# Keeping w1 in its load tiles across the layer-1 forward and backward products, and shorter lives for wq and K tiles in the layer-1 backward attention

## The chip, the core and the metric

The kernel runs on one core of a Trainium2 chip. The metric is device time in microseconds of one launch. Times inside the program are given from the start of the profiled span.

## The reference, cut to what matters

Two layers are applied to a decode step of 2 sequences (D = 1024): attention over a cache of 16384 positions (32 query heads, 4 key/value heads, head size 128), then an MLP (F = 3584, tanh Gelu), each with a residual. Both layers use the same weights. The output and the gradients with respect to x, both caches and all weights are returned.

```python
x = A_x
x = x + _A_ref(_layernorm(x, axis=-1), A_k_cache, A_v_cache, A_wq, A_wo)
x = x + _B_ref(_layernorm(x, axis=-1), B_w1, B_b1, B_w2, B_b2)
x = x + _A_ref(_layernorm(x, axis=-1), A_k_cache, A_v_cache, A_wq, A_wo)
x = x + _B_ref(_layernorm(x, axis=-1), B_w1, B_b1, B_w2, B_b2)
```

_B_ref applies a second layer norm of its own, then h = gelu(y @ w1 + b1) and h @ w2 + b2. The backward pass needs, in layer 1, dh = (g @ w2.T) * gelu', then dh @ w1.T, two layer-norm backwards, the product with wo.T, the attention backward, the product with wq.T, and the same again for layer 0.

## The kernel before, in words

The two caches are 64 MB in all (2 sequences x 4 heads = 8 groups of 4 MB for K and as much for V), so they are streamed from memory. The unit of loading is a tile of 128 partitions x 4096 bf16, 1 MB. The pool `ld` has NLD = 7 such tiles. All loads are issued by the queue of SyncE (SP) in the order of the program (`w_take` L331 for weights, `kv_load` L469 for the caches, L961 and L986 for wq). A new tile takes, of the 7 buffers, the one whose last reader stands earliest in the program; its load waits on SP until that reader is done, and all loads after it on SP wait too. The order of every engine's instructions is written out by hand (the kernel opens a manual schedule); nothing is moved by a scheduler.

The stages follow each other: layer 0 forward, layer 1 forward, layer 1 backward, layer 0 backward with the output gradients.

Weights. `w_fwd` (L341) multiplies a vector by a weight matrix: it loads the tiles one by one and, on each, has PE make 32 small matmuls (`fwd_rows` L337) into the accumulator `acc_all`. w1 has 7 tiles (6 of 4 x 1024 columns, one of 8 x 512). The class `Back` (L361) multiplies by the transposed matrix. Its `load(k)` (L371) loads tile k and leaves four units in `todo[k]`; a unit turns a quarter of the tile in place, either on DVE (`turn32` L269, a transpose of 32 x 32 blocks, for rows below `nd`) or on PE (`turn` L358: eight 128 x 128 transposes into a PSUM tile, then a copy back by ACT, L159). `some(k, n)` runs n units, `prod(k)` the products of tile k (`products` L296 behind DVE-turned rows into `dm_d`, L418 behind PE-turned ones into `dm_p`), and `run()` goes over the tiles, turning tile k + 1 before the products of tile k. `open` makes the spread operand from dh (`spread_g` L278 and L281). `copies_on("A")` puts PSUM copies on ACT.

The layer-1 MLP. `mlp_hidden(1)` runs two layer norms, `w_fwd` over w1 (7 loads), adds b1 (`hpre` L830) and computes the Gelu (L832 to L846: Exp on ACT at L838, the rest on DVE). `mlp_slope(1)` (L859 to L869) computes the derivative of the Gelu, `mlp_hidden_bwd` (L874) dh. `weights_down(1)` (L876) then loads the 7 tiles of w1 again as a `Back`, multiplies, loads wo (8 tiles, also a `Back`), runs the two layer-norm backwards and multiplies by wo.

The layer-1 backward attention, `attn_bwd` (L645). It walks over slots; a slot is a quarter (8 x 128 positions) of a V tile: PE transposes it (`emit_T` L480), a copy brings it to SBUF, and two slots later PE makes dP from it (`score`, L726). After four slots `post` makes dS of the chunk on DVE (L698) and puts the products with the K tile of the same chunk into a queue: `quad` (L512), two halves for each K tile, each taken in a later slot. A K tile is loaded when its first quad is issued, except in the last group (index 6): there `post` loads it at once (`accs[g].pre[c] = kv_load(...)`), and at the last chunk `post` also issues the loads of the first five w2 tiles of the next stage (`ahead.load(k)`).

When both sequences of a key/value head are done, `wq_now` queues the product with that quarter of wq: in the next slot both its tiles are loaded, in slots +7 to +14 DVE turns them row by row, in slots +12 and +17 PE multiplies (L296), at +19 the sums are collected. The last quarter of wq (`wq_steps`, `wqL` below is its pair of tiles) is loaded and turned on PE from the second slot of the last group on, one step in every other slot (more often when over six wait), and multiplied at the very end (`products` L995), as its dq is known only then. The order of groups is 0, 4, 3, 1, 5, 2, 6, with group 7 (its tiles are held) in between; there are 128 slots, 112 to 127 being the last group. In the idle slots after the last V tile, units of w2 tile 0 are run (`ahead.some(0, 1)`).

After it come the product with w2 for layer 0 (`w2b`: a forward product for layer 1 and a transposed one in one pass), w1 and wo again, and the layer-0 attention backward with all stores.

## Time and profile before

| what | value |
|---|---|
| median of 3 runs | 1139.64 us (1136.17 to 1146.07) |
| profiled execution: span on the page (a time of its own beside the span is not given) | 1138.1 us |
| PE busy | 915.9 us, 80% |
| DVE, ACT busy | 619.8 us (54%), 534.0 us (47%) |
| POOL busy | 70.2 us, 6% |
| moved by DMA | 449.20 MB, mean 395 GB/s |
| read, written | 348.14 MB, 98.58 MB |
| chain that ended last, by engine | PE 45%, DMA 35%, DVE 10%, issue 5%, ACT 4% |
| loads of w1 and w2 tiles (in_B_w) | 42 of 1 MB, median 12.9 us to landing |

The page gives busy time for each engine, the span in 40 slices of 28.45 us, the DMA queues, and the chain of work that ended last: followed back from the last instruction, at each step to whatever released it. Busy shares are averages over all stages, so the stages that the change touches are read from the stretches and the timeline: layer-1 w1 lies at about 421 to 469 us, the layer-1 backward attention at about 490 to 666 us. A DMA's time in the chain runs from its issue to its landing and so holds the wait behind other transfers. In the timeline, the bracket at the end of a line is the idle time of that engine before the instruction and what ended it.

### The profile page before, as it was taken

How to read it: one execution, taken by the hardware profiler on the slowest of the kernel's cores; microseconds unless marked ns; L12 is line 12 of the kernel's file. 1: busy time of each engine (PE TensorE's matmuls, PEld its weight loads, DVE VectorE, ACT ScalarE, POOL GpSimd, SP SyncE). 2: the span in 40 equal slices, each digit the busy share in tenths (PEclk: the TensorE clock that was granted, in tenths of full speed). 3: DMA queues.
4: the chain of work that ended last, by engine and by line, in shares of the span. 5: the costliest groups of instructions: out<-in, count | busy, mean ns of one | idle time of the engine just before them, and what ended most of it. 6: DMA issues, size and time to landing. Idle time of an engine off the chain costs nothing.

```text
span 1138.1 us, 38123 instructions
## 1 busy us (share of the span) xinstructions
PE 915.9 (80%) x16766; PEld 674.7 (59%) x16767; DVE 619.8 (54%) x1363; ACT 534.0 (47%) x1356; POOL 70.2 (6%) x124
## 2 busy tenths in 40 slices
PE   4979795468888975789887678888898897899996
PEld 3867674358766754778765567755545454455552
DVE  1545451180545523654442246678798767786876
ACT  0544351005544420434333214468697766676764
POOL 0000000000000000000000000022121111111210
PEclk9988895567999875899998678999999978897978
DMA  8999999999999979999999699998999999999997
GB/s 371 423 425 425 424 424 413 395 413 423 423 425 423 412 288 404 388 422 421 399 413 393 232 380 309 370 386 302 403 419 421 421 419 424 423 411 421 423 385 290
DMA packets 104183, 449.20 MB, mean 395 GB/s; under 512 B 7238, under 2 KB 11334, under 8 KB 66896
## 3 DMA queue, kind: packets, MB, share of 16 engines
q1 hardware_dynamic: 86672, 354.46, 77.6%
q0 software_dynamic: 17344, 92.29, 19.6%
q8 instruction: 131, 2.15, 0.7%
q14 instruction: 36, 0.29, 0.1%
HBM read 348.14 MB, written 98.58 MB: 393 GB/s over the span
## 4 chain that ended last, share of the span: by engine, by line
PE 45%; DMA 35%; DVE 10%; issue 5%; ACT 4%; POOL 0%; SPq 0%; DVEq 0%; ACTq 0%; POOLq 0%
DMA kv_V<-in_A_v_cache_dram 13%; PE tp L480 10%; DMA wt<-in_B_w_dram 5%; PE acc_all L512 4%; PE tpm L1527 4%; DMA kv_K<-in_A_k_cache_dram 4%; PE xm L1336 4%; DMA wt<-in_A_wo_dram 3%; DMA out_dram<-keepK 3%; DMA keepK<-in_A_v_cache_dram 3%; PE sc L633 3%; PE xm L1250 2%; PE wtp L358 2%; PE dp L1389 2%; PE dp L726 2%
## 5 line engine op out<-in xcount | busy, mean ns | idle before, releaser
L159 ACT COPY kT<-tp 128x512 int32<-128x512 int32 x200 | 117.4, 587 | 298.4 <-PE tp L480 289.1
L162 DVE COPY kT<-tp 128x1024 bf16<-128x1024 bf16 x168 | 114.9, 690 | 141.8 <-PE tp L480 130.4
L480 PE MATMUL tp<-ident,kv_K 128*128 128x128 bf16 x1728 | 142.0, 230 | 6.9 <-DMA kv_K<-in_A_k_cache_dram 6.8
L480 PEld LDWEIGHTS <-kv_K 128*128 128x128 bf16 x1728 | 107.8, 103 | 7.7 <-DMA kv_K<-in_A_k_cache_dram 7.5
L170 DVE CAST big<-xm 128x512 bf16<-128x512 f32 x133 | 86.3, 684 | 19.3 <-PE xm L1336 14.3
L167 ACT CAST big<-xm 128x512 bf16<-128x512 f32 x151 | 82.1, 595 | 25.0 <-PE xm L1336 14.8
L633 PE MATMUL sc<-qT_bf,kT 128*128 128x8 bf16 x2048 | 91.5, 171 | 0.1
L633 PEld LDWEIGHTS <-kT 128*128 128x128 bf16 x2048 | 75.7, 97 | 26.7 <-issue 20.8
L337 PEld LDWEIGHTS <-wt 128*128 128x128 bf16 x1920 | 57.4, 104 | 54.7 <-issue 17.8
L167 ACT CAST keepV<-xm 128x512 bf16<-128x512 f32 (+1 forms) x137 | 75.0, 594 | 29.5 <-PE xm L1336 18.5
L480 PE MATMUL tp<-ident,kv_V 128*128 128x128 bf16 x864 | 70.2, 227 | 14.1 <-DMA kv_V<-in_A_v_cache_dram 12.2
L597 ACT ACTIVATE e_all<-sc,negm 128x64 bf16<-128x64 f32 x256 | 77.2, 343 | 1.0 <-DVE negm L592 1.0
L170 DVE CAST keepV<-xm 128x512 bf16<-128x512 f32 (+1 forms) x101 | 65.9, 684 | 18.9 <-PE xm L1336 12.7
L269 DVE STREAM_TRANSPOSE wt<-wt 128x512 int32<-128x512 int32 x104 | 63.6, 674 | 14.2 <-PE w2b_f L337 11.0
L512 PE MATMUL acc_all<-kv_V,e_all 128*16 128x256 bf16 x864 | 46.0, 293 | 28.7 <-DMA kv_V<-in_A_v_cache_dram 14.4
L159 ACT COPY wt<-wtp 128x512 int32<-128x512 int32 x72 | 40.3, 587 | 57.0 <-PE wtp L358 54.1
L480 PEld LDWEIGHTS <-kv_V 128*128 128x128 bf16 x864 | 55.2, 101 | 16.2 <-DMA kv_V<-in_A_v_cache_dram 13.1
L597 ACT ACTIVATION_READ_ACCUMULATOR e_all<-sc,negm 128x1 f32 x256 | 59.8, 234 | 0.0
L167 ACT CAST keepK<-xm 128x512 bf16<-128x512 f32 x98 | 53.0, 596 | 14.1 <-PE xm L1336 7.5
L1389 PE MATMUL dp<-wdo,kT 128*128 128x64 bf16 x896 | 52.8, 206 | 0.0
L358 PE MATMUL wtp<-ident,wt 128*128 128x128 bf16 x576 | 47.8, 244 | 4.9 <-ACT wt L159 2.6
L1336 PE MATMUL xm<-QmK,blk 64*128 64x512 bf16 x256 | 48.8, 444 | 2.3 <-ACT keepV L167 1.0
(387 smaller groups left out, 1564.4 us busy)
## 6 DMA issues: line engine op xcount, KB each, us to landing
kv_K<-in_A_k_cache_dram SPq DMA_DIRECT2D x81, 1024.0 KB, 13.0
kv_V<-in_A_v_cache_dram SPq DMA_DIRECT2D x81, 1024.0 KB, 12.9
wt<-in_B_w_dram SPq DMA_DIRECT2D x42, 1024.0 KB, 12.9
wt<-in_A_wo_dram SPq DMA_DIRECT2D x32, 1024.0 KB, 9.6
out_dram<-big POOLq DMA_DIRECT2D x26, 1024.0 KB, 18.9
out_dram<-keepV POOLq DMA_DIRECT2D x19, 1024.0 KB, 20.7
out_dram<-keepK POOLq DMA_DIRECT2D x17, 1024.0 KB, 17.8
wt<-in_A_wq_dram SPq DMA_DIRECT2D x16, 1024.0 KB, 11.0
```

Source lines behind the costliest of these rows:

```text
L159: S.copy(out=dst.bitcast(I32), in_=src.bitcast(I32))
L162: V.tensor_copy(out=dst, in_=src)
L167: S.copy(out=dst, in_=src)
L170: V.tensor_copy(out=dst, in_=src)
L269: V.transpose(out=w, in_=w)
L358: PE.transpose(tp[:, o, :], view[:, o * 128:(o + 1) * 128], ident[:])
L480: PE.transpose(tp[:, j, :], cv[:, b * 8 + j, :], ident[:])
L512: PE.matmul(self.acc[cg:cg + 16, :], lhsT=coef(u), rhs=self.cv[:, t:t + 2, :].rearrange("p t d -> p (t d)"), start=False, stop=True, tile_ ...
L597: S.activation(out=e_all[:, g, f * half:(f + 1) * half, l, h, :], in_=sc[g][f][:, h, :].rearrange("p (a b) -> p a b", b=2), func=ACT.Exp, ...
L633: PE.matmul(sc[g][f][:, :, t % TH], lhsT=kT[:, j, :], rhs=q_bf[:, g, :], start=True, stop=True)
L1336: PE.matmul(pss[k][:], lhsT=blk[p:p + 64, o + 2 * h + k // 2, :], rhs=Qm[p:p + 64, :, :].rearrange("p a b -> p (a b)"), start=True, stop=T ...
L1389: PE.matmul(dp[:, :, t:t + 4], lhsT=kT[:, j, :], rhs=wd[:, :, x:x + 4], start=(b + j == 0), stop=False)
```

## The change

Three things are changed.

1. w1 is loaded once for layer 1. `mlp_hidden(1)` gets the `Back` object; `w_fwd` with `keep` loads all 7 tiles through it, and after the forward product of tile k runs the turning units of tile k (all four, for the first six; for the last tile the two PE-turned ones, and its two DVE-turned ones later, one beside the Exp and one after the spread). Forward products go over the tiles in the order 1, 0, 3, 2, 5, 4, 6. `weights_down(1)` finds the tiles loaded and turned. The seven buffers are held from the loads to the products.
2. The Gelu of layer 1 and its derivative are computed in one chain that uses the square and 0.5 (1 + th) once; the write of `h_all` for layer 1 (`h1_out`) stands after the start of the backward product.
3. In `attn_bwd` the two wq tiles of a quarter are loaded four slots apart and each is turned and multiplied in the slots right after (slots +1/+4 to +7/+9 and +5/+8 to +11/+13, sum at +15); the last quarter is begun seven slots later and taken one step a slot; K tiles of the last group are loaded at their first quad; the five w2 loads stand in the queue behind the last K quad; one unit of w2 tile 0 stands ahead of the last wq product, the others follow after the attention.

```diff
--- before.py
+++ after.py
@@ -338,11 +338,22 @@
                           rhs=x[:, j0 + j, :].unsqueeze(1).to_broadcast([128, nw // 2, 2]),
                           start=False, stop=True, skip_group_check=True)
 
-    def w_fwd(W, n_in, n_out, x, between=None):
+    def w_fwd(W, n_in, n_out, x, between=None, keep=None):
         JO = n_out // 128
         nw = min(WIDE, 512 // JO)
         fps = ACCT[:, 0:JO * nw].rearrange("p (j b) -> p j b", b=nw)
         V.memset(fps, 0.0)
+        if keep is not None:
+            keep.fps, keep.x, keep.nw = fps, x, nw
+            for k in range(len(keep.tiles)):
+                keep.load(k)
+            for k in range(len(keep.tiles)):
+                keep.forward(k)
+                if k < len(keep.tiles) - 1:
+                    keep.some(k)
+            for _ in range(2):
+                keep.todo[k].pop()()
+            return fps[:, :, 0:2]
         for j0, nj, c0, cw in w_tiles(W, n_in, n_out):
             fwd_rows(fps, nw, w_take(W, j0, nj, c0, cw), x, j0, c0 // 128)
             if between:
@@ -367,6 +378,11 @@
             self.tiles = [tiles[i] for i in order]
             self.n_o, self.wv, self.todo = n_out // 128, {}, {}
             self.seen = set()
+            self.nw = None
+
+        def forward(self, k):
+            j0, nj, c0, cw = self.tiles[k]
+            fwd_rows(self.fps, self.nw, self.wv[k], self.x, j0, c0 // 128)
 
         def load(self, k):
             j0, nj, c0, cw = self.tiles[k]
@@ -374,7 +390,7 @@
             flat, per = wv.rearrange("p j n -> p (j n)"), max(1, 1024 // cw)
 
             def unit(u):
-                if self.fps is not None:
+                if self.fps is not None and self.nw is None:
                     fwd_rows(self.fps, WIDE, wv[:, u:u + 1], self.x, j0 + u, 0)
                 if j0 + u * per < self.nd:
                     turn32(flat[:, u * 1024:(u + 1) * 1024])
@@ -673,14 +689,13 @@
         def wq_now(kv):
             n = wq_job(kv)
             n[1]()
-            for f in n[0]:
-                sch.later(1, f)
-            for j in range(DJ):
-                sch.later(7 + j, n[2][j])
             for k in range(2):
-                sch.later(12 + 5 * k, n[3][k])
+                sch.later(1 + 4 * k, n[0][k])
+                for j in range(4):
+                    sch.later(4 + 4 * k + j, n[2][4 * k + j])
+                sch.later(9 + 4 * k, n[3][k])
             if kv == groups[-3] % HKV:
-                sch.later(19, wq_sum)
+                sch.later(15, wq_sum)
 
         def wq_sum():
             fin = px([128, DJ, 2], F32, "dn_fin")
@@ -704,18 +719,21 @@
                     done_g.append(g % HKV)
                     if g == groups[-1]:
                         wq_n["last"][1]()
+                        ahead.some(0, 1)
                         wq_n["last"][3]()
                     elif done_g.count(g % HKV) == 2:
                         wq_now(g % HKV)
                 accs[g] = Acc(g, "K", None, finish, 2 if g == G - 1 else groups.index(g) % 2)
             acc = accs[g]
-            if g == groups[-1]:
-                accs[g].pre[c] = kv_load("K", g, c)
+            coef = lambda u: ds[:, u - c * CP].rearrange("p h t -> p (h t)")
+            def queue():
+                queue_acc(sch, acc, [c], False, coef)
+                if g == groups[-1] and c == NCH - 1:
+                    sch.q.append(lambda: [ahead.load(k) for k in range(NLD - 2)])
                 if c == NCH - 1:
-                    for k in range(NLD - 2):
-                        ahead.load(k)
-            coef = lambda u: ds[:, u - c * CP].rearrange("p h t -> p (h t)")
-            sch.later(2, lambda: queue_acc(sch, acc, [c], c == NCH - 1, coef))
+                    queue_acc(sch, acc, [], True)
+
+            sch.later(1 if g == groups[-1] else 2, queue)
 
         def score(s):
             g, c, b = slots[s]
@@ -745,7 +763,7 @@
                     kTs[s] = emit_T(cv, b, True)
                     if s % 3 == 2 and s >= 8 and v_turns:
                         v_turns.popleft()()
-                if g == groups[-1] and b == 1 and c == 0:
+                if g == groups[-1] and b == 0 and c == 2:
                     n = wq_n["last"] = wq_steps(l, g % HKV, dqT, dn, lambda: pt([128, 8, 128], BF16, "wtq"),
                                                 lambda: px([128, 512], F32, "dn_ps"))
                     for k, f in enumerate(n[0]):
@@ -754,10 +772,8 @@
             sch.run_slot(1 if s < len(slots) else 2)
             if 2 <= s < len(slots) + 2:
                 score(s - 2)
-            if wq_q and (s % 2 == 1 or len(wq_q) > 6):
+            if wq_q:
                 wq_q.popleft()()
-            if s > len(slots) + 2:
-                ahead.some(0, 1)
             s += 1
         assert not wq_q
 
@@ -821,11 +837,15 @@
         saved[f"a{l}"] = dict(y=y, rstd=rstd, qT_bf=qT_bf, rbc=rbc, oT=oT)
         return xn
 
-    def mlp_hidden(l, xT):
+    def mlp_hidden(l, xT, keep=None):
         y1, rstd1 = ln_fwd(xT[:], f"m{l}a")
         y2, rstd2 = ln_fwd(y1[:], f"m{l}b")
         V.tensor_copy(out=m_all[:, 0:DJ, lsl(l)], in_=y2[:])
-        hps = w_fwd(B_w1, D, F, m_all[:, 0:DJ, lsl(l)])
+        if keep is not None:
+            copies_on("A")
+        hps = w_fwd(B_w1, D, F, m_all[:, 0:DJ, lsl(l)], keep=keep)
+        if keep is not None:
+            copies_on(None)
         hpre = vec.tile([128, FJ, 2], F32, name=f"hpre{l}")
         V.tensor_tensor(out=hpre[:], in0=hps, in1=b1T[:].to_broadcast([128, FJ, 2]), op=ALU.add)
         x2 = wrk.tile([128, FJ, 2], F32, name="g_x2")
@@ -836,6 +856,11 @@
         V.tensor_tensor(out=u[:], in0=w_[:], in1=hpre[:], op=ALU.mult)
         z = wrk.tile([128, FJ, 2], F32, name="g_z")
         S.activation(out=z[:], in_=u[:], func=ACT.Exp, scale=2.0 * GELU_C)
+        if keep is not None:
+            V.tensor_scalar(out=x2[:], in0=x2[:], scalar1=3.0 * GELU_A * GELU_C * 0.5, scalar2=GELU_C * 0.5,
+                            op0=ALU.mult, op1=ALU.add)
+            V.tensor_tensor(out=x2[:], in0=x2[:], in1=hpre[:], op=ALU.mult)
+            keep.some(len(keep.tiles) - 1, 1)
         V.tensor_scalar(out=z[:], in0=z[:], scalar1=1.0, scalar2=None, op0=ALU.add)
         rz = wrk.tile([128, FJ, 2], F32, name="g_rz")
         V.reciprocal(out=rz[:], in_=z[:])
@@ -843,8 +868,20 @@
         V.tensor_scalar(out=th[:], in0=rz[:], scalar1=-2.0, scalar2=1.0, op0=ALU.mult, op1=ALU.add)
         hh = wrk.tile([128, FJ, 2], F32, name="g_hh")
         V.tensor_scalar(out=hh[:], in0=th[:], scalar1=1.0, scalar2=0.5, op0=ALU.add, op1=ALU.mult)
-        V.tensor_tensor(out=h_all[:, 0:FJ, lsl(l)], in0=hh[:], in1=hpre[:], op=ALU.mult)
-        saved[f"m{l}"] = dict(y1=y1, rstd1=rstd1, y2=y2, rstd2=rstd2, hpre=hpre, th=th, xT=xT)
+        d1 = None
+        if keep is not None:
+            t2 = wrk.tile([128, FJ, 2], F32, name="gb_t2", tag="g_z")
+            V.tensor_tensor(out=t2[:], in0=th[:], in1=th[:], op=ALU.mult)
+            V.tensor_scalar(out=t2[:], in0=t2[:], scalar1=-1.0, scalar2=1.0, op0=ALU.mult, op1=ALU.add)
+            V.tensor_tensor(out=x2[:], in0=x2[:], in1=t2[:], op=ALU.mult)
+            d1 = vec.tile([128, FJ, 2], F32, name=f"gb_d1{l}")
+            V.tensor_tensor(out=d1[:], in0=hh[:], in1=x2[:], op=ALU.add)
+            hidden_after = lambda: V.tensor_tensor(out=h_all[:, 0:FJ, lsl(l)], in0=hh[:], in1=hpre[:], op=ALU.mult)
+        else:
+            hidden_after = None
+            V.tensor_tensor(out=h_all[:, 0:FJ, lsl(l)], in0=hh[:], in1=hpre[:], op=ALU.mult)
+        saved[f"m{l}"] = dict(y1=y1, rstd1=rstd1, y2=y2, rstd2=rstd2, hpre=hpre, th=th, xT=xT, w1=keep, d1=d1)
+        return hidden_after
 
     def mlp_out(l, fps):
         xn = vec.tile([128, DJ, 2], F32, name=f"xM{l}")
@@ -873,14 +910,22 @@
         for p, ap in dhps:
             V.tensor_tensor(out=dh_all[:, p, lsl(l)], in0=d1[:, p], in1=ap, op=ALU.mult)
 
+    def w1_back():
+        return Back(B_w1, D, F, 4, [1, 0, 3, 2, 5, 4, 6], "dm")
+
     def weights_down(l, gT, name, mid=None):
         sv = saved[f"m{l}"]
-        w1b = Back(B_w1, D, F, 4, [1, 0, 3, 2, 5, 4, 6], "dm")
-        for k in range(len(w1b.tiles)):
-            w1b.load(k)
+        w1b = sv.pop("w1", None)
+        if w1b is None:
+            w1b = w1_back()
+            for k in range(len(w1b.tiles)):
+                w1b.load(k)
         w1b.banks()
         w1b.open(dh_all[:, 0:FJ, lsl(l)])
         copies_on("A")
+        if l == 1:
+            w1b.some(len(w1b.tiles) - 1)
+            h1_out()
         w1b.some(0)
         w1b.run(mid)
         wob = Back(A_wo, HD, D, 16, [4, 5, 0, 1, 6, 2, 3, 7], "do")
@@ -1045,9 +1090,7 @@
         V.tensor_copy(out=dh_up1[:], in_=dh_fin[:])
 
     x3 = attn_layer_fwd(1, x2_, deque([lambda: w2a_turn(NW2 - 1, 0, 2), lambda: w2a_turn(NW2 - 1, 2, 4), w2a_end]))
-    mlp_hidden(1, x3)
-    mlp_slope(1)
-
+    h1_out = mlp_hidden(1, x3, w1_back())
     mlp_hidden_bwd(1, [(slice(0, FJ), dh_up1[:])])
     g3, do_ps = weights_down(1, gT4, "1")
     do1 = attn_out_bwd(1, do_ps)
```

## Prediction

> **What bounds the kernel now.** I read the page's slices first, then the stages in stretches of 4 us, then the chain that ended last, then the timeline of the two places that the change touches.
>
> ```profile
> DMA  8999999999999979999999699998999999999997
> GB/s 371 423 425 425 424 424 413 395 413 423 423 425 423 412 288 404 388 422 421 399 413 393 232 380 309 370 386 302 403 419 421 421 419 424 423 411 421 423 385 290
> ```
>
> A slice is 28.45 us. Where the kernel runs well it moves 420 to 425 GB/s with the DMA engines full, so time is bytes over 420 GB/s; a 1 MB tile (1.0486 MB) takes 2.5 us, a weight tile at the 404 GB/s of its stretches 2.6 us. The weak slices count: the 23rd (626 to 654 us) has 232 GB/s. It is the end of the layer-1 backward attention. Then the stretches (columns: us, busy of PE, PEld, DVE, ACT, POOL, granted clock, DMA share, GB/s):
>
> ```profile
> 444.00:448.00 4.00, 1.02 (x32) 1.03 (x33) 1.47 (x6) 0.25 (x1) 0.00 (x0) 0.50 1.05 404
> 448.00:452.00 4.00, 1.38 (x28) 1.35 (x28) 3.59 (x18) 0.09 (x1) 0.00 (x0) 0.50 1.05 407
> ...
> 616.00:620.00 4.00, 3.75 (x49) 2.97 (x47) 1.02 (x2) 0.82 (x2) 0.00 (x0) 0.50 1.01 423
> 620.00:624.00 4.00, 4.00 (x71) 3.22 (x68) 1.55 (x3) 1.52 (x3) 0.00 (x0) 0.77 0.87 307
> 624.00:628.00 4.00, 2.01 (x41) 1.79 (x41) 3.95 (x9) 1.75 (x3) 0.00 (x0) 1.00 0.94 314
> 628.00:632.00 4.00, 1.99 (x32) 1.47 (x32) 0.66 (x2) 0.34 (x1) 0.00 (x0) 0.59 0.69 268
> 632.00:636.00 4.00, 1.03 (x8) 0.77 (x8) 0.00 (x0) 0.83 (x2) 0.00 (x0) 0.50 0.75 262
> 636.00:640.00 4.00, 3.75 (x73) 3.13 (x74) 0.00 (x0) 0.65 (x2) 0.00 (x0) 0.50 0.23 37
> 640.00:644.00 4.00, 3.43 (x51) 3.19 (x48) 1.73 (x3) 2.51 (x5) 0.00 (x0) 0.71 0.96 399
> 644.00:648.00 4.00, 1.13 (x10) 1.13 (x10) 0.00 (x0) 0.05 (x1) 0.00 (x0) 0.72 0.87 344
> 648.00:652.00 4.00, 4.00 (x73) 3.08 (x73) 0.95 (x3) 0.59 (x1) 0.00 (x0) 0.50 0.02 10
> 652.00:656.00 4.00, 3.87 (x87) 2.86 (x86) 1.56 (x4) 1.17 (x2) 0.00 (x0) 0.93 0.88 286
> ```
>
> Around w1 the DMA is full at 404 to 407 GB/s while the other engines idle. In the nine stretches from 620 to 656 it moved 2227 of the 9 x 420 = 3780 (GB/s summed over stretches of 4 us): 1553 x 4 / 420 = 14.8 us of transfer time lost, and no engine is busy throughout either. The chain shows that loads end it, each issued only just before:
>
> ```profile
> 622.16 7.58 DMA kv_K<-in_A_k_cache_dram
> ...
> 631.60 4.61 DMA kv_V<-in_A_v_cache_dram
> ...
> 638.72 8.10 DMA kv_V<-in_A_v_cache_dram
> ...
> 653.54 6.65 DMA wt<-in_B_w_dram
> ```
>
> A lone load takes 4.6 us from issue (the one at 631.60), so a load issued when its reader is next is exposed. Why so late: a new load tile takes the buffer whose last reader stands earliest in the program, of 7. Counted in the order of the program at the load of V chunk 2 of the last group (slot 120): two wq tiles of kv 1, two of the last quarter, one preloaded K, the K in use: 6 of 7 live. That load is issued at 631.60, as the last transpose of V chunk 1 ends (630.55 + 1.01).
>
> **Part 1: w1 kept.** Removed: 7 loads of 1 MB, 7.34 MB at 404 GB/s = 18.2 us of a full DMA queue, and two DVE operations (hpre squared again 0.21, the second 0.5(1+th) 0.18). Turning is moved, not removed: 14 PE/ACT units and 14 DVE units of each 512 int32 columns.
>
> Forward, in the time base of before. The 7 tiles land as now, 2.6 us apart, the last at 445.0; m_all lets PE start at 436.36. A forward tile costs 0.88 us (160 matmuls in 4.41). A PE-turned tile costs 3.59 at clock 0.50 (timeline, 450.84) and about 2.5 at 1.00 (4 units, ACT 0.59 each plus hand-over). The clock rises after a stretch of 3.41 us in which PE is busy throughout (451.26 to 454.67: 3.41 busy, 1.00 from there); 437.6 to 441.0 becomes such a one. So: 436.4 + 0.9 + 3.5 = 440.8; two forwards 442.6; turn 445.1; two forwards 446.9; turn 449.4; two forwards 451.2. New wait: hpre stands on DVE behind the four turns of tile 5, which start after its forward (450.3) and take 2.49: 452.8. The Gelu and slope now form one chain: 15 small DVE operations, the Exp on ACT and one turn of 0.62 partly beside it, about 4.35 us (now 4.5, 446.07 to 450.57, with two operations more and no turn). dh is ready at 457.15, now 450.57: 6.6 us later. But no turn is left between the products: spread 0.28, four dm_p at 0.97 to 1.25, dm_d at 0.63 to 1.02, together 8.5 half cold, end 465.7 against 468.72. PE chain: -3.0.
>
> DMA: nothing can be loaded from 445.0 until the first product frees a tile (458.7, as the wo loads stand behind it on SP); a lone load takes 4.6 us, so wo flows from about 460.9. Idle 15.9 against 18.2 saved, and the dip that before has at 478.56 to 481.98 (284 GB/s, 1.0 us) goes: -3.3. The ln chain (8.3 us) and wo turns behind it are as before and shift along; the K/V stream after it is DMA-full to 544, so the shift survives. I take **-3**. Bounds: all turns hidden, dh at 453.5, -7; all turns and products cold and the wo start late, +2.
>
> Here the Trainium skill speaks against the change: Trainium Kernel Development and Optimization, Best Practices, asks to double-buffer and overlap DMA with compute, and seven held tiles give that up. By the rule alone the reload was hidden and free, the 15.9 us idle is pure loss, and the whole sum would end near 1141. The row decides otherwise: at 404 GB/s the reload had nothing to hide behind.
>
> **Part 2: shorter tiles at the end.** Bytes are equal. The wq loads of kv 1 go from both at slot 109 to slots 109 and 113 and are let go at 117 and 121 (before 120 and 125); the last quarter's load at 120 and 124 (before 113 and 119); K tiles of the last group are taken at their first use, not at post; the w2b loads stand behind the last K, as before. Live tiles at any load are now 3 of 7 at most, so each load can be issued 5 to 9 slots ahead of its reader. Example: V chunk 2 takes the buffer of a K tile released in slot 114, six slots ahead.
>
> The landings then follow the DMA: the first wq tile of kv 1 is down at 607.8 (now the second wq tile and then a V follow, and that V is waited for until 612.88, two tiles later); 15 tiles behind it stands the first w2b tile, in both versions: 607.8 + 15 x 2.5 + 5 weight tiles x 0.1 = 645.8. Now it lands at 660.24. **-14.4.** Is PE a tighter limit? From 612.8, all cold (T 0.81 x 16, dp 0.24 x 16, quads 0.55 x 14, wq rows 0.83 x 8, two products 1.0, dS waits 0.4 x 4, reduce 1.0): 36 us, last quad 649; warm at about 0.6 of that it waits for DMA. Before, that quad ends 662.0, so even cold it is 13 earlier. Behind it: the last K lands 643.2, its quads end 643.9, evacuation, reduce and dq 2.0, the one w2b unit 0.4, products and dn 2.1: 648.4; then the three w2b units no longer done early put 3 x 0.62 = 1.9 us of DVE turns ahead of the layer-norm (5.6 us from dn to gM_all, now 3.4). On that chain gM_all comes at 654.0 instead of 669.5, -15.5; the stream is the tighter, and both feed a stage that is DMA-full at 402 to 412 from 660 to 672. New waits on PE: row 4 of the last quarter waits for its load (635.3), with transposes and quads queued behind; it is inside the count. Bounds: half of the loss, -7.2, if transfers in flight share the rate and the needed one lands late (the K issued at 622.16 took 7.58); -15.5 at best. Splitting the earlier wq pairs may also mend the dip at 544 to 548 (287 GB/s, 1.3 us): I count 0, bound -1.3. POOL issues nothing here.
>
> **Sum.** -3 - 14.4 = -17.4. The profiled span is 1138.1, inside the three runs, 1.5 under their median; the span would be 1120.7 and the time 1139.64 - 17.4 = 1122.2.
>
> **Rivals.** (1) w1 gives nothing back: its turns stay cold (2 x 1.1 more) and so do the products (1.0 more). For it: 437.6 to 441.0 with 3.17 busy stayed at 0.50. Against: the turns leave PE no gap. that eats the 3: 1139.64 - 14.4 + 0.2 = 1125.4. (2) Only half of the tail is won, for the shared rate above: 1139.64 - 3 - 7.2 = 1129.4. (3) Slower: dropping the K preload exposes every load of the tail. If each came as the lone one at 631.60, 4.6 us, the first w2b tile would land at 607.8 + 15 x 4.6 = 677, 17 late: 1139.64 + 17 - 3 = 1154. It decides from (660.24 + 3 - 607.8) / 15 = 3.7 us a tile; against it stand the free buffers, 4 of 7. (4) No effect, because the loss is taken up by a wait that I don't see behind 660: 1139.6.
>
> **How the numbers follow.** Forecast 0.52, own range 1117 (-7 and -15.5) to 1127 (w1 at 0, the cold PE's -13); rival 1 0.22; rival 2 0.16; rival 3 0.06; rival 4 0.04. A measurement of this kernel tells about 1%, 11.4 us, from no change: faster is below 1128.2, forecast and rival 1, 0.74; same is rivals 2 and 4, 0.20; slower rival 3, 0.06. Range: low 1139.64 - 7 - 15.5 - 1.3 = 1115.8, taken as 1115; high rival 2 with w1 at nothing, 1132.4, taken as 1132; outside are rivals 3 and 4 and the ends, 0.15.
>
> **What would show it.** Right: 7 B_w loads fewer; a DMA hole of 14 to 17 us after the layer-1 w1 loads; dh some 6 us later, dm_sb some 3 earlier; over 400 GB/s through the last group, no load waited for over 2 us, the first w2b tile 14 us earlier against the group's start. Wrong: a hole over 20 us; K or V waits of 3 to 4 us left at the end; PE busy throughout at clock 0.50 there.

## The result, and the profile after

The changed kernel takes 1123.03 us (median; 1121.06 to 1124.98) against 1138.89 us (1136.17 to 1146.07) for the kernel before, measured beside it: a ratio of 0.9845 with a 95% interval of 0.9819 to 0.9871, 15.9 us less. In two later sessions the same kernel stood at 0.9825 [0.9802, 0.9849] and 0.9836 [0.9802, 0.9870]. The profiled execution's own time is 1123.85 us, its span 1122.1 us. 1122.2 us was forecast.

The slices of the page of the changed kernel, in the same form as before (28.05 us each now):

```profile
DMA  8999999999999987799999999998999999999997
GB/s 370 423 424 425 425 424 415 398 414 419 422 411 424 418 316 302 265 416 407 377 416 418 396 381 346 377 365 308 411 373 421 423 419 424 424 417 422 422 411 284
```

Two things moved. The slice with 232 GB/s has gone: the 23rd is now at 396. And two slices have become weak, the 16th and 17th (302 and 265, before 404 and 388; the 15th was weak already): this is the stage in which w1 is held. So the change trades one hole for another, and each has to be looked at in stretches of 4 us (columns: us, busy time of PE, PEld, DVE, ACT, POOL, granted clock, DMA share, GB/s):

```profile
444.00:448.00 4.00, 3.77 (x104) 3.65 (x102) 2.49 (x4) 2.33 (x5) 0.00 (x0) 1.00 0.17 57
448.00:452.00 4.00, 2.58 (x82) 2.50 (x80) 3.55 (x11) 2.03 (x5) 0.00 (x0) 1.00 0.02 4
452.00:456.00 4.00, 1.14 (x48) 1.14 (x47) 3.66 (x14) 0.00 (x0) 0.00 (x0) 0.68 0.00 0
456.00:460.00 4.00, 4.00 (x166) 3.88 (x163) 1.16 (x4) 0.00 (x0) 0.00 (x0) 0.50 0.50 174
```

From 444 to 460 the DMA moved 57 + 4 + 0 + 174 = 235 (GB/s summed over the four stretches) of the 404 + 407 + 409 + 396 = 1616 that the same stretches moved before: 1381 x 4 / 404 = 13.7 us of transfer time are lost, against 18.2 us of loads saved. The list of the waits of SP's queue, between 440 and 660 us, says why (columns: total us, times, longest):

```profile
SPq L331 <- PE dm_p L434: 23.3, 4, 20.7
```

The loads of wo (L331) stand behind the first product with w1 (dm_p), since all seven buffers hold w1 until then: one wait of 20.7 us. It does no harm by itself: the wo tiles are wanted only after two layer-norm backwards, and between 455 and 492 us PE waits for no load. What counts is when the chain of the other engines ends:

```profile
450.73 0.18 DVE L850 TENSOR_TENSOR hpre<-acc_all,b1T 128x56 f32<-128x56 f32 x1
...
454.55 0.22 DVE L911 TENSOR_TENSOR dh_all<-gb_d,dh_up 128x56 bf16<-128x56 f32 x1
...
465.35 0.17 DVE L937 COPY dm_sb<-dm_f 128x8 f32<-128x8 f32 x1 [0.46 <-PE dm_f L308]
```

This is the timeline of DVE. In the kernel before, the last two of these stand at

```profile
450.35 0.22 DVE L874 TENSOR_TENSOR dh_all<-gb_d,dh_up 128x56 bf16<-128x56 f32 x1
...
469.01 0.17 DVE L892 COPY dm_sb<-dm_f 128x8 f32<-128x8 f32 x1 [0.45 <-PE dm_f L308]
```

So dh is ready 4.2 us later than before, and dm_sb (the result of the products with w1) 3.66 us earlier.

The end of the attention in stretches, to be held against 616 to 656 us of the kernel before:

```profile
620.00:624.00 4.00, 3.71 (x74) 2.67 (x75) 0.00 (x0) 1.17 (x2) 0.00 (x0) 0.59 1.04 406
...
628.00:632.00 4.00, 3.85 (x97) 3.44 (x94) 1.49 (x4) 2.24 (x4) 0.00 (x0) 1.00 1.01 403
632.00:636.00 4.00, 2.94 (x64) 2.68 (x65) 1.94 (x5) 0.61 (x2) 0.00 (x0) 1.00 1.05 431
636.00:640.00 4.00, 3.85 (x81) 3.37 (x78) 1.72 (x3) 2.26 (x4) 0.00 (x0) 1.00 0.91 386
...
644.00:648.00 4.00, 2.99 (x100) 2.90 (x99) 1.51 (x6) 0.00 (x0) 0.00 (x0) 0.58 0.99 335
```

There is no stretch with 37 or 10 GB/s any more; the least of 616 to 656 us, 335, is the last one shown. And the chain that ended last, followed through the same place:

```profile
617.58 10.19 DMA wqt<-in_A_wq_dram
...
638.01 7.34 DMA wt<-in_B_w_dram
645.40 0.40 PE w2b_f L337 x8
645.79 1.71 PE dn_ps L1040 x64
...
647.75 1.90 DVE wt L269 x3
```

Before, the chain ran here from one K or V load to the next; now PE's rows lie between the load of 617.58 and that of 638.01. The first w2 tile is down at 645.40 (before 660.24), and the three turns of w2 that were done early before stand on the chain with 1.90 us.

### The profile page after: what moved, and what is told of

Its sections match the earlier page's. It is cut to its first block, busy times and chain, and to the rows that moved or that the text cites. A ratio compares the mean times of both kernels' runs of the same rounds, so it can differ in the third digit from the quotient of the medians.

```text
span 1122.1 us, 38104 instructions
## 1 busy us (share of the span) xinstructions
PE 916.9 (82%) x16766; PEld 678.3 (60%) x16767; DVE 619.1 (55%) x1362; ACT 532.6 (47%) x1355; POOL 70.1 (6%) x124
## 4 chain that ended last, share of the span: by engine, by line
PE 33%; DMA 14%; DVE 8%; issue 4%; ACT 3%; POOL 0%; DVEq 0%; ACTq 0%; SPq 0%; POOLq 0%
PE tpm L1570 4%; PE tp L496 4%; PE xm L1379 3%; DMA keepK<-in_A_v_cache_dram 3%; PE wtp L369 3%; DMA out_dram<-keepK 3%; PE xm L1293 3%; DMA kv_K<-in_A_k_cache_dram 2%; PE dp L1432 2%; PE acc_all L528 2%; PE dp L744 2%; DMA out_dram<-keepxV 2%; DMA wt<-in_B_w_dram 2%; DVE wt L269 1%; DVE keepV L170 1%
## 5 line engine op out<-in xcount | busy, mean ns | idle before, releaser
L496 PE MATMUL tp<-ident,kv_K 128*128 128x128 bf16 x1728 | 147.8, 236 | 4.4 <-DMA kv_K<-in_A_k_cache_dram 4.4
L496 PEld LDWEIGHTS <-kv_K 128*128 128x128 bf16 x1728 | 112.2, 105 | 5.1 <-DMA kv_K<-in_A_k_cache_dram 4.9
L170 DVE CAST keepV<-xm 128x512 bf16<-128x512 f32 (+1 forms) x101 | 66.1, 685 | 19.6 <-PE xm L1379 12.9
L170 DVE CAST keepK<-xm 128x512 bf16<-128x512 f32 x69 | 44.8, 684 | 8.5 <-PE xm L1379 5.1
## 6 DMA issues: line engine op xcount, KB each, us to landing
kv_K<-in_A_k_cache_dram SPq DMA_DIRECT2D x81, 1024.0 KB, 12.9
out_dram<-keepK POOLq DMA_DIRECT2D x17, 1024.0 KB, 17.6
```

The lines of the kernel that those rows point to most:

```text
L170: V.tensor_copy(out=dst, in_=src)
L496: PE.transpose(tp[:, j, :], cv[:, b * 8 + j, :], ident[:])
```

## The experiments

For each run the table gives the median time, the ratio to the kernel before in the same session with its interval, and four marks from the profiled execution, in us: when dm_sb of layer 1 is written; when the 26th of the 32 dS operations (dX on DVE) begins, shortly before the last group; when gM_all of layer 1 is written, behind that group; and the time between the last two, called the tail.

| run | us | ratio | dm_sb | 26th dS | gM_all | tail |
|---|---|---|---|---|---|---|
| before (first session) | 1138.89 | 1 | 469.01 | 602.19 | 669.35 | 67.16 |
| changed | 1123.03 | 0.9845 [0.9819, 0.9871] | 465.35 | 601.08 | 652.65 | 51.57 |
| whole_again | 1120.40 | 0.9825 [0.9802, 0.9849] | 465.59 | 598.67 | 650.26 | 51.59 |
| whole_third | 1122.57 | 0.9836 [0.9802, 0.9870] | 465.94 | 600.55 | 652.16 | 51.61 |
| w1_only | 1136.54 | 0.9950 [0.9925, 0.9976] | 466.21 | 601.70 | 666.21 | 64.51 |
| attn_only | 1124.91 | 0.9848 [0.9815, 0.9880] | 468.65 | 605.01 | 653.78 | 48.77 |
| attn_alone2 | 1124.69 | 0.9854 [0.9821, 0.9887] | 469.15 | 605.90 | 656.30 | 50.40 |
| k_early | 1122.24 | 0.9817 [0.9789, 0.9845] | 465.20 | 598.54 | 652.28 | 53.74 |
| pair_early | 1124.14 | 0.9839 [0.9809, 0.9868] | 465.50 | 598.82 | 652.42 | 53.60 |
| last_early | 1126.27 | 0.9880 [0.9861, 0.9900] | 466.22 | 600.69 | 656.70 | 56.01 |
| only_last | 1127.72 | 0.9872 [0.9837, 0.9907] | 466.47 | 600.06 | 656.68 | 56.62 |
| only_pair | 1129.44 | 0.9919 [0.9891, 0.9947] | 464.18 | 598.84 | 657.52 | 58.68 |
| none3 | 1136.28 | 0.9972 [0.9956, 0.9989] | 464.91 | 600.37 | 665.12 | 64.75 |
| turn_later | 1116.33 | 0.9781 [0.9746, 0.9817] | 460.86 | 595.42 | 646.60 | 51.18 |

The sessions were: w1_only, attn_only, k_early, pair_early; whole_again, last_early, only_pair, none3; whole_third, attn_alone2, turn_later, only_last. In them the kernel before took 1143.75, 1138.91 and 1140.51 us; the first two rows are from the result's own session. Times of one session are compared with each other. The first of the three has no run of the changed kernel, so its runs are held against that kernel by the ratios.

The marks come from one execution each. The tail of the changed kernel agrees within 0.04 us in its three executions, but attn_only and attn_alone2, which are the same program, differ by 1.6 us. The two ends of the tail, in the kernel before and in the changed one:

```profile
602.19 0.42 DVE L698 TENSOR_TENSOR dX<-dp,e_all 128x256 bf16<-128x256 f32 x1 [4.25 <-PE dp L692]
669.35 0.17 DVE L1071 CAST gM_all<-gA 128x16 bf16<-128x16 f32 x1
...
601.08 0.42 DVE L713 TENSOR_TENSOR dX<-dp,e_all 128x256 bf16<-128x256 f32 x1 [0.63 <-PE dp L707]
652.65 0.17 DVE L1114 CAST gM_all<-gA 128x16 bf16<-128x16 f32 x1
```

### Each half alone

Theory A: the two halves add up, 3 us from w1 and 14.4 from the attention. Rival B: w1's lead is eaten by PE before the tail, and the attention alone is nearly everything.

w1_only is the changed kernel with `attn_bwd` as it was before:

```diff
+            for f in n[0]:
+                sch.later(1, f)
...
-            if wq_q:
+            if wq_q and (s % 2 == 1 or len(wq_q) > 6):
                 wq_q.popleft()()
+            if s > len(slots) + 2:
+                ahead.some(0, 1)
```

> The w1 and Gelu parts of the change alone, the layer-1 backward attention as before. Theory A (the parts add up as forecast): the 3 us won at dm_sb last to the end, time 3 us under the kernel before, ratio about 0.997. Theory B (from the trace of the changed kernel: its dS marks lead by 3.4 us at 495, by 1.9 from 500 to 545 and by 0 to 1 from 558 to 600, so the lead is eaten by PE before the tail): dm_sb 3.5 us earlier, the first dS of the attention 3.4 earlier, the dS marks of the last group within 1.5 us of those before, time 0 to 1.5 us under the kernel before, ratio 0.999 to 1.000.

attn_only is the kernel before with the changed kernel's `attn_bwd`:

```diff
-            for f in n[0]:
-                sch.later(1, f)
...
-            if wq_q and (s % 2 == 1 or len(wq_q) > 6):
+            if wq_q:
                 wq_q.popleft()()
-            if s > len(slots) + 2:
-                ahead.some(0, 1)
```

> The attention part of the change alone, w1 loaded twice as before. Theory A: the first w2 tile of the next stage is waited for until about 646 instead of 660, time 14.4 us under the kernel before, ratio 0.987. Theory B: nearly the whole of the change's 16 us, time 14.5 to 16 under, ratio 0.986, within 1.5 us of the whole change. Rival 3 of the prediction (dropping the preload exposes the loads, and w1 paid for it) would give a ratio over 0.99.

Measured: w1 alone gives 0.9950, which is 2.7 to 8.6 us of its session's 1143.75 and takes in A's 3 us but not B's 0 to 1.5; the attention alone gives 0.9848, with an interval that takes in both A's 0.987 and B's 0.986. Both halves gain by themselves, and together they gain no more than the sum. That w1 gives something by itself is shown; how much of it is left beside the attention's gain was not, so the pair was run again in one session.

The changed kernel itself twice more, as the measure for its neighbours:

> The whole change once more, beside the next three kernels on one chip. All theories: ratio to the kernel before 0.984 to 0.986, 16 to 18 us under it.

> The changed kernel once more, as the measure for the other three on one chip. Both theories: 0.982 to 0.985 of the time before.

And attn_only's kernel a second time, beside whole_third:

> w1 loaded twice, as before; only the attention part of the change. Theory A (w1's lead of 3.7 us at dm_sb is kept to the end): 3 to 4 us slower than the whole change, 0.985 to 0.988 of the time before. Theory B (the lead is eaten in the PE-bound stretch between 490 and 560 us): within 1 us of the whole change, 0.982 to 0.985.

Measured: 1124.69 us against 1122.57 us, 2.1 us for w1, with intervals that overlap (0.9821 to 0.9887 and 0.9802 to 0.9870). This lies between A's 3 to 4 us and B's 1 us, and the times alone do not tell 3 from 0 here. The marks say where the lead is: 3.2 us at dm_sb, 5.3 at the 26th dS, 4.1 at gM_all. It was to be settled by making the lead larger, which turn_later below does.

### Which of the three shortenings

Theory L: a load costs time only where its buffer comes free within about four slots of its reader, so one shortening can be undone for nothing. Rival S: each carries a share of 4 to 5 us.

k_early loads the K tiles of the last group when `post` runs, as before:

```diff
             acc = accs[g]
+            if g == groups[-1]:
+                accs[g].pre[c] = kv_load("K", g, c)
```

> The whole change, but the K tiles of the last group are loaded at the post of their chunk again, as before. Counted in the order of the program, at most 5 of the 7 buffers are then live at a load of the last group (3 in the change, 6 before). Theory L (what costs is only a load with one buffer or none free): the same time as the whole change within 2 us. Theory S (each of the three shortenings carries a share of the 15 us): 4 to 5 us slower than the whole change, ratio to the kernel before 0.989.

pair_early takes back the splitting of the wq pairs:

```diff
+            for f in n[0]:
+                sch.later(1, f)
+            for j in range(DJ):
+                sch.later(7 + j, n[2][j])
             for k in range(2):
-                sch.later(1 + 4 * k, n[0][k])
-                for j in range(4):
-                    sch.later(4 + 4 * k + j, n[2][4 * k + j])
-                sch.later(9 + 4 * k, n[3][k])
+                sch.later(12 + 5 * k, n[3][k])
             if kv == groups[-3] % HKV:
-                sch.later(15, wq_sum)
+                sch.later(19, wq_sum)
```

> The whole change, but both wq tiles of a finished quarter are loaded together in the next slot and multiplied in slots +12 and +17 again, as before. At most 4 buffers are live at a load of the last group. Theory L: within 2 us of the whole change. Theory S: 4 to 5 us slower than it, ratio to the kernel before about 0.989.

last_early begins the last wq quarter where it was begun before:

```diff
-                if g == groups[-1] and b == 0 and c == 2:
+                if g == groups[-1] and b == 1 and c == 0:
...
-            if wq_q:
+            if wq_q and (s % 2 == 1 or len(wq_q) > 6):
```

> The whole change, but the last quarter of wq is begun in the second slot of the last group and taken a step every other slot, as before. Counted in the order of the program, the buffer of every load of the last group is let go at least 4 slots ahead of its reader (5 in the whole change, 1 in the kernel before), and at most 4 of 7 buffers are live. Theory L (a load costs only when its buffer comes free within about a lone load's 4.6 us, some 4 slots, of its reader): within 2 us of the whole change. Theory S (each of the three shortenings carries a share): 4 to 5 us slower than the whole change.

only_pair undoes K and the last quarter, so that only the split pair is left (both edits above together):

```diff
+            if g == groups[-1]:
+                accs[g].pre[c] = kv_load("K", g, c)
...
-                if g == groups[-1] and b == 0 and c == 2:
+                if g == groups[-1] and b == 1 and c == 0:
...
-            if wq_q:
+            if wq_q and (s % 2 == 1 or len(wq_q) > 6):
```

> Of the three shortenings only the split of the wq pairs is left: the K tiles of the last group are loaded at the post and the last quarter of wq begins early, as before. Buffers are let go 3 slots ahead for four loads and 2 for one, at most 5 live. Theory L: 3 slots are 3 to 4 us against 4.6 to 7.5 from issue to landing, so four loads expose 1 to 3 us each: 4 to 8 us slower than the whole change. Theory S: 9 to 10 us slower.

none3 undoes all three; w1 is kept, and the five w2 loads stay behind the last K quad:

```diff
+            for f in n[0]:
+                sch.later(1, f)
...
+            if g == groups[-1]:
+                accs[g].pre[c] = kv_load("K", g, c)
...
-                if g == groups[-1] and b == 0 and c == 2:
+                if g == groups[-1] and b == 1 and c == 0:
...
-            if wq_q:
+            if wq_q and (s % 2 == 1 or len(wq_q) > 6):
```

> All three shortenings undone; left of the attention part are only that the w2 loads are queued behind the last K quad and the order around the last wq product. w1 is kept. Buffers are let go 1 slot ahead of their reader for two loads, with 6 of 7 live, as in the kernel before. Both theories: 11 to 15 us slower than the whole change, near the kernel with the w1 part alone (ratio 0.995). If it were as fast as the whole change, the gain would come from the moved w2 loads.

Measured, as the tail against 51.6 us of the whole change: K +2.1, pair +2.0, last +4.4, K and last +7.1, all three +13.2. In time, against whole_again: last +5.9 us, K and last +9.0, all three +15.9. For K and pair alone the ratios (0.9817 and 0.9839) cannot be told from the whole change's. L holds for K and for the pair in the times, and falls at the last quarter, which was to be free and is not. S is right on K and last together (9 to 10 us expected), but falls on the single sizes, and because all three cost more than their sum: 2.1 + 2.0 + 4.4 = 8.5 us one by one, 13.2 together. The 2.1 and 2.0 are little more than the 1.6 us between two executions of one program, and the times of only_pair spread from 1126.14 to 1134.36. A fourth combination was added to see whether the last quarter is the thing itself or whether it is free buffers:

> The whole change with the pair of wq loads and the K preload put back as before; only the later start of the last wq quarter is left of the three shortenings. Theory F (free buffers decide, and any two of the three put back make loads late): 8 to 10 us slower than the whole change, 0.990 to 0.993. Theory O (what decides is that the last quarter's first turn stands in PE's order at once behind its load, with K and V quads behind it; the other two are nothing): within 2 us of the whole change, 0.982 to 0.986.

```diff
+            for f in n[0]:
+                sch.later(1, f)
...
+            if g == groups[-1]:
+                accs[g].pre[c] = kv_load("K", g, c)
```

Measured: 5.2 us slower than whole_third, tail +5.0. Neither theory of that run holds: O wanted under 2, F 8 to 10. K and pair, each within the noise of the times, cost 5 together. So no single one of the three is the cause. Two at a time cost about their sum (5.0 against 4.1, 7.1 against 6.5; pair and last together were not run); only with all three undone is the price clearly higher. The reading offered is that each tile kept longer takes free buffers from the loads behind it, and that the price rises as they run out.

What the price consists of is seen on PE and DMA. PE's waits for loads between 600 and 664 us (total, times, longest), in the kernel before:

```profile
PE tp L480 <- DMA kv_V<-in_A_v_cache_dram: 10.9, 3, 4.6
PE acc_all L512 <- DMA kv_K<-in_A_k_cache_dram: 5.2, 2, 3.8
```

in the changed kernel:

```profile
PE tp L496 <- DMA kv_V<-in_A_v_cache_dram: 3.6, 3, 1.8
PE acc_all L528 <- DMA kv_K<-in_A_k_cache_dram: 2.7, 4, 1.4
...
PE wtq L369 <- DMA wqt<-in_A_wq_dram: 0.4, 1, 0.4
```

and in none3, where the old waits are back, though the w2 loads stand where the change puts them:

```profile
PE tp L496 <- DMA kv_V<-in_A_v_cache_dram: 11.0, 4, 4.4
PE acc_all L528 <- DMA kv_K<-in_A_k_cache_dram: 5.5, 3, 3.1
```

PE's waits for K, V and wq tiles in this window rank nearly as the tails do: 6.7 us in the changed kernel, 7.8 in k_early, 8.8 in pair_early, 10.2 in last_early, 11.2 in only_last, 11.9 in only_pair, 17.6 in none3 and 16.9 before. In last_early, though, the V and K waits are those of the changed kernel (3.8 and 2.7 us); what is new is 3.7 us at the turns of wq, most of it here:

```profile
617.11 1.03 PE L369 MATMUL wtq<-ident,wqt 128*128 128x128 bf16 x8 [2.77 <-DMA wqt<-in_A_wq_dram]
```

That load had been issued at 601.78, 15.28 us before it landed, so its buffer had come free by then; the DMA was moving 397 to 429 GB/s from 604 to 616 us, with other loads ahead of it, and its turn stood next in PE's order. So the last quarter's price begins with its own load, read too soon, and not with buffers alone.

The stretches of none3 show the holes, too (last two columns):

```profile
628.00:632.00 4.00, 2.72 (x40) 2.15 (x39) 0.00 (x0) 1.05 (x2) 0.00 (x0) 0.53 0.70 225
632.00:636.00 4.00, 1.61 (x36) 1.42 (x40) 0.00 (x0) 0.66 (x2) 0.00 (x0) 0.50 0.39 164
...
644.00:648.00 4.00, 2.94 (x35) 2.50 (x36) 0.86 (x2) 0.00 (x0) 0.00 (x0) 0.66 0.37 158
648.00:652.00 4.00, 4.00 (x69) 2.95 (x67) 0.73 (x2) 1.17 (x2) 0.00 (x0) 0.50 0.41 123
```

DMA is busy for 0.70, 0.39, 0.37 and 0.41 of them, and PE idles in three of the four: a load waits for a buffer, PE waits for the load, and the buffer waits for PE. Counting in the order of the program how many slots lie between a buffer's last reader and the slot that loads into it again, from slot 108 on and for the tiles of the attention: at least 5 for every load in the changed kernel, at least 4 with any one shortening undone, down to 2 in only_last and only_pair, 1 in none3 and in the kernel before. This is a count on the program, not a measurement; a run with the old lives and more buffers, which would test the buffers by themselves, was not made.

### w1: the turns moved further

If theory A holds, a larger lead at dm_sb has to reach the end; under B it does not. turn_later takes the turns that are needed last out of the way of hpre: the PE turns of the fifth and the last tile run beside the Gelu (the last tile's two stood behind the last forward product already); of the four DVE turns of the sixth tile one follows its forward, one stands beside the Gelu and two beside the products, as do the last tile's two.

```diff
                 keep.forward(k)
-                if k < len(keep.tiles) - 1:
+                if k < 4:
                     keep.some(k)
-            for _ in range(2):
-                keep.todo[k].pop()()
+                if k == 5:
+                    keep.some(5, 1)
+            keep.some(4, 1)
...
-            keep.some(len(keep.tiles) - 1, 1)
+            copies_on("A")
+            keep.some(4)
+            for _ in range(2):
+                keep.todo[6].pop()()
+            copies_on(None)
+            keep.some(5, 1)
...
-            w1b.some(len(w1b.tiles) - 1)
             h1_out()
```

> The whole change, with the PE turns of the fifth w1 tile and of the last one put beside the Gelu instead of ahead of its input, and three of the four DVE turns of the sixth tile beside the products. The last forward product should end at about 446.5 instead of 449.7 us, dh come 3 to 3.5 us earlier and dm_sb 3 to 4 us earlier (461.5 to 462.5 instead of 465.4). Theory A: the time falls by as much, 0.979 to 0.982. Theory B: dm_sb is earlier all the same, but the time stays within 1 us of the whole change.

Measured: 1116.33 us (1114.57 to 1118.26) against 1122.57 us (1120.88 to 1125.94) of whole_third: 6.2 us faster, the fastest of all versions, 0.9781 [0.9746, 0.9817] of the time before. DVE's timeline:

```profile
447.55 0.21 DVE L851 TENSOR_TENSOR hpre<-acc_all,b1T 128x56 f32<-128x56 f32 x1
...
451.41 0.22 DVE L917 TENSOR_TENSOR dh_all<-gb_d,dh_up 128x56 bf16<-128x56 f32 x1
...
460.86 0.17 DVE L942 COPY dm_sb<-dm_f 128x8 f32<-128x8 f32 x1 [0.47 <-PE dm_f L308]
```

hpre is about 1 us later than worked out, as PE reaches the last four forwards only at 444.15 and ends them at 447.5. dh comes 3.1 us earlier than in the changed kernel and dm_sb 4.5. The 1.4 us that dm_sb gains on dh come from the products: PE idles for only 0.50 us ahead of the spread, and the granted clock is 1.00 from 452 to 456 us. On PE's timeline of turn_later the first product behind DVE-turned rows is

```profile
452.90 0.63 PE L296 MATMUL dm_d<-wt,Gw 128*8 128x128 bf16 x32
```

and on that of the changed kernel, after 4.24 us of idle PE and at clock 0.50,

```profile
456.10 1.02 PE L296 MATMUL dm_d<-wt,Gw 128*8 128x128 bf16 x32
```

The lead over whole_third is 5.1 us at dm_sb and at the 26th dS, 5.6 at gM_all, 6.2 in the time, more than the 3 to 4 us that A expected. So A holds here: a lead of 5 us from the w1 stage passes through the attention to the end, and B falls. That the changed kernel's own lead of 3 us passes as well is inferred from this; the times do not resolve it.

## Why the prediction was right, point by point

The total: -17.4 us forecast; by the medians -15.9, then -18.5 and -17.9 in the later sessions. The likeliest case was the one that came, and as far as the runs resolve the two parts, the sum did not come out right by errors that cancel across them.

The tail, -14.4 by the stream and -15.5 by PE's chain: the tail of the table fell from 67.16 to 51.57, 51.59 and 51.61, by 15.6; the first w2 tile landed at 645.40 where 645.8 was forecast. That landing was worked out for a stage that starts as before, and at the 26th dS the profiled execution was 1.1 us ahead, so that part of the agreement is luck: for a start 1.1 us earlier the landing is 0.7 us late. whole_again, 3.5 us ahead at the 26th dS, has it at 642.81, 0.5 us late in the same sense. How much belongs to the attention depends on what it is held against: beside w1 it is 64.51 - 51.6 = 12.9 us, without w1 67.16 - 50.40 = 16.8 and 67.16 - 48.77 = 18.4; the forecast lies between. The tail flatters the attention alone, as its 26th dS begins 2.8 and 3.7 us later than before; its gM_all is 15.6 and 13.1 us earlier. That the three shortenings are the whole of it is shown by none3: with them undone, and nothing else, its tail is 64.75, near the 64.51 of w1_only, and the w2 loads and units that were moved give nothing that can be seen. That free buffers are the reason rests on the count and on the waits, and for the last quarter they are not the only one. In the sum by PE's chain, 5.6 us from dn to gM_all should read 5.3 (3.4 + 1.9); 5.1 were measured (647.54 to 652.65). Three details did not come: the stream runs at over 400 GB/s only until 636 us, then at 386, 350 and 335; row 4 of the last quarter does not wait for its load (the only wait of wtq is 0.4 us, on row 0), and PE, cold at 0.50 to 0.59 in parts of the tail, was no tighter limit, since it found the clock at 0.98 to 1.00 from 624 to 644.

w1, -3 us: dm_sb -3.66 us; in time 2.1 us beside the attention's part, with intervals that overlap, and alone 2.7 to 8.6 us in w1_only and 1.3 to 5.0 in none3, whose tail is that of w1_only. Two terms under it were mis-sized and cancel. The turns cost less: two forwards and a PE turn repeat every 3.8 us (440.29, 444.11, 447.92) where 4.3 was forecast, so dh came 4.2 us late instead of 6.6. The products cost more: from dh to dm_sb 465.35 - 454.55 = 10.8 us, against 8.5. Their clock was 0.50 from 456 to 460 instead of half cold, and the gap of 2.32 us that the last section shows was not in the sum. The DMA hole is 13.7 us, forecast 15.9, as dh was earlier. From hpre to the end of dh it is 4.04 us (forecast 4.35, before 4.50), so the merged Gelu and slope can account for some 0.5 us of the lead; no run has that part by itself.

"The K/V stream after it is DMA-full to 544, so the shift survives" was the weak step. The conclusion holds, as turn_later shows; the reason is not good. Before, PE is as full as DMA there (500 to 504 us: PE 3.90 of 4.00 at 424 GB/s). In the changed kernel from 496 to 512 us PE is busy for 15.88 of 16 us and DMA moves only 390 GB/s: there PE sets the pace, and a lead can be lost on it. In the profiled execution 1.45 us were, between the first dS (3.42 us ahead of before) and the second (1.97). whole_again, the same program, was 3.47 and 3.46 ahead. The last section shows what differs.

The dip at 544 to 548 us, counted at nothing: right; 291 GB/s after, 287 before.

The rivals. Rival 1 (w1 gives nothing) falls for w1 by itself with w1_only, whose interval lies below 1; beside the attention's part the case against it is turn_later, whose lead reaches the end. Rival 2 (half of the tail) falls: the tail gave 15.6. Its mechanism, transfers in flight that share the rate, is there (the w2 load of 638.01 takes 7.34 us, where the lone one before took 4.61) but was in the landing times already. Rival 3 (no K preload exposes every load) is the one that k_early tests: with the preload back the tail is 2.1 us longer, not shorter, so the preload buys nothing. Rival 4 (a wait behind 660 takes it up) falls: from gM_all to the end of the span it is 468.75 us before and 469.45 after.

The Trainium skill's rule weighed in the forecast, to double-buffer and overlap DMA with compute (Trainium Kernel Development and Optimization, Best Practices), speaks against holding all seven tiles. The rule alone gave 1141 for the whole change; w1_only, where the held tiles stand without the attention's part (but with the merged Gelu), measures 0.9950 [0.9925, 0.9976]. Here the measurement decides for holding them.

## What to carry to other kernels

Where a stage moves less than full DMA rate while PE waits for loads, count for each load, in the order of the program, how long before its reader its buffer comes free; shorten the lives of tiles that are loaded early and read late, and do it for all of them, since undoing all three cost more than the sum (2.1, 2.0 and 4.4 us one by one, 13.2 together). A tile that is read in the slot of its own load can be waited for even when its buffer is free in time, because other transfers are ahead of it (15.28 us from issue to landing in last_early). When tiles are kept to save their reload, the work that is done on them while they are held belongs beside the chain, not ahead of it: moving four PE turns and three DVE turns behind the input of the Gelu was worth another 6.2 us. A lead is only worth what the stages after it pass on, so test it by making it larger rather than by measuring it at the limit of the noise.

## What the runs showed of the hardware that was not expected

The granted clock falls at the start of the attention in some executions and not in others of the same program. The stretches of the changed kernel around the fall:

```profile
490.99:494.40 3.41, 1.79 (x45) 1.78 (x46) 2.35 (x9) 0.58 (x1) 0.00 (x0) 1.00 1.03 432
494.40:497.81 3.41, 3.41 (x48) 3.40 (x45) 1.50 (x4) 1.17 (x2) 0.00 (x0) 0.51 1.01 418
```

PE is busy throughout in the second stretch and runs at half clock for all of its 3.41 us; it had been busy for 1.79 of the 3.41 us before. The same shows in whole_third (493.23 to 496.64), turn_later (489.55 to 492.96) and attn_alone2 (497.07 to 500.48), and not in whole_again or before, whose clock stays at 1.00 from 478 to 512 us. From dm_sb to the second dS these four executions lose 1.5 to 1.9 us against the kernel before, and whole_again loses nothing. Such a fall is one reason why a lead of 3 us is hard to see in the times. The Trainium skill, TensorE: Matmul & The Clock Gate, Part 1, describes a free-running window of about 3.4 us, which agrees with the 3.41 us of these rows; it lets the clock fall after an idle window, while here a window in which the profile shows PE busy for 52% was enough (43 to 48% in the other three).

PE stands still for over 2 us in the middle of the w1 products, waiting for nothing that the profile shows, and at the same place in every version. In the changed kernel:

```profile
460.12 0.69 PE L296 MATMUL dm_d<-wt,Gw 128*8 128x128 bf16 x29
463.14 0.23 PE L296 MATMUL dm_d<-wt,Gw 128*8 128x128 bf16 x3 [2.32 <-issue]
```

Before it was 2.30 us, in turn_later 2.04, in none3 3.32. It lies on the chain to dm_sb. In every trace it comes after the same number of recorded PE instructions, 15297, nearly all matmuls and weight loads, and a 16 KB transfer of the kind that the profile lists as instruction starts close to it: at 460.87 us in the changed kernel and at 464.69 before, just after PE's last matmul has started, and in turn_later at 456.19, just ahead of it. That points to the fetch of instructions, but PE does not stop at each of the 131 such transfers, and no run tried it, so the cause stays open.
